# Loading q and k cast, in 14-token pieces, and splitting the score and value PSUM tiles, in an attention kernel with a gated convolution

## The chip, the cores and the metric

The kernel runs on one core of a Trainium2 chip. The metric is the device time of one execution in microseconds (us); lower is better. Times of one kernel vary by about 1% between executions, so kernels that are compared here ran in turn on the same chip, in rounds with the kernel before. Executions at a lower granted TensorE clock or over 1.5% above the fastest of the same kernel count as slow and are left out of the ratios.

Engine names in the profile: PE is TensorE's matmuls and PEld its weight loads, ACT is ScalarE, DVE is VectorE, POOL is GpSimd, SP is SyncE, which issues most transfers. L235 is a line of the kernel's source.

## The reference

Causal attention with 8 batches, 12 heads, 448 tokens and head size 64, then a causal convolution of 5 taps along the tokens as a gate, a value product, and an output product (cut to what matters):

```python
scores = (q @ k.transpose(0, 1, 3, 2)) / sqrt(64)
attn = softmax(where(causal_mask, -1e9, scores))
x = (attn @ v) as [batch, token, head * 64]          # 768 features
gate = sigmoid(sum(conv_w[t] * x shifted by 4 - t for t in range(5)))
out = (gate * (x @ w_val)) @ w_out                    # float32, 8 x 448 x 768
```

## The kernel before

Work goes in 24 groups of four heads (3 groups a batch). Iteration `n` of the main loop computes the scores of group `n`, and the value products, normalisation and convolution of group `n - 1`. From the fourth iteration it also computes a third of the value product of the batch before (`val`), and from the seventh two or three output projections (`next_out`). The engines run their own instruction streams in program order; a semaphore holds an instruction until the tiles that it touches are free or filled.

q and k come in fp32 by whole batches, in 512-byte pieces (two tokens of 64 values), and GpSimd casts them to bf16. A bf16 pair is one 32-bit word, and DVE transposes 32 x 32 blocks of words:

```python
nc.sync.dma_start(out=qk_f[name, b][32 * j:32 * (j + 1), g0:g1].rearrange("p g a c -> p (g a) c"),
                  in_=src[b, h + g0:h + g1].rearrange("h (a p u) d -> p (h a) (u d)", a=7, u=2))
...
nc.gpsimd.tensor_copy(out=t, in_=qk_f[name, n // NG][:, n % NG])                 # cast
...
nc.vector.transpose(out=t.bitcast(U32).rearrange("p (a b u) -> p a u b", u=2, b=32), in_=...)
```

PSUM has one score tile of four banks and one value tile of two:

```python
sc_ps = ps.tile([128, G, 512], FP32, name="sc_ps")     # a bank for each of the four heads
av_ps = ps.tile([128, 2, 512], FP32, name="av_ps")     # a bank for each half of the features
```

The exponential reads the score banks in two instructions of two heads, the convolution of group `n - 1` then reuses the first two banks, and the value product of the batch before reuses `av_ps`:

```python
for hp in range(2):
    nc.scalar.activation(out=pt[:, 2 * hp:2 * hp + 2, ...], in_=sc_ps[:, 2 * hp:2 * hp + 2], func=AF.Exp, scale=D ** -0.5)
...
conv(n - 1, sc_ps[:, 0:2])
...
val(b - 1, g, av_ps)          # 12 matmuls, then one DVE instruction over both halves
```

The main loop, in its order (cut):

```python
for n in range(N + 1):
    load_v(n + 2); ...                       # q and k of the next batches
    # n = 0, 1: 12 loads each of the value weights; n = 2 to 4: 8 each of the output weights (GpSimd)
    # n = 2: DVE reorders all the value weights (order_w)
    scores(n, 0); softmax_numerators(n, 0)   # exponentials, then causal masks on GpSimd
    attend(n - 1)                            # denominators, then value products
    next_out(b - 2, z_ps)
    scores(n, 1); softmax_numerators(n, 1)
    normalize(n - 1)
    next_out(b - 2, den_ps)
    conv(n - 1, sc_ps[:, 0:2])
    ...
    transposes(n + 1); cast_v(n + 1); cast_qk(n + 2)
    val(b - 1, g, av_ps)
```

The softmax here doesn't subtract the row's maximum and nothing guards it: scores larger than these inputs give would overflow.

## Time and profile before

| | before |
|---|---|
| time, median of 2 runs | 291.25 us |
| PE busy | 223.7 us, 77% of the span of 291.6 us |
| start of the convolution of group 1 | 47.88 us |
| groups 5 to 22, a convolution to the next (median) | 9.44 us |
| after the convolution of group 22 | 39.2 us |

The start of each group's convolution is a convenient mark: there is one for each of the 24 groups, and PE executes it in order. Below, "second convolution" is that of group 1. Of the 17 steps from group 5 to 22, two hold one projection more and take 10.4 us, so the 17 take 162.48 us in all. The profiled execution took 293.33 us, 2 us more than the median.

The profile's page, the chain that ended last and the timeline are shown in the prediction. Three rows of its list of waits hold the kernel's three losses. A row has who waited, for whom, the sum in us, how often, and the longest wait:

```profile
PE sc_ps L235 <- ACT pt L184: 25.4, 22, 2.0
PE den_ps L208 <- POOL pt L188: 11.0, 2, 5.8
...
DVE wp L109 <- DMA wv<-in_moe_w_val_dram: 12.0, 3, 6.5
```

The first is the convolution waiting for exponentials: often and short, so it belongs to the steady part. The others are a few long waits, at the start: denominators for masks, and the reordering of the value weights for their transfer.

### The profile page before, as it was taken

Reading aid. Unit: us, or ns where it says so; the run is one execution under the profiler, and the core shown is the slowest. Engines: PE = TensorE matmul, PEld = TensorE weight load, DVE = VectorE, ACT = ScalarE, POOL = GpSimd, SP = SyncE. Lnnn points to the kernel's source line nnn. Section 1 sums busy time; section 2 is a strip of 40 time slices with the busy share of each in tenths; the row PEclk is TensorE's granted clock in tenths of the full one; section 3 lists DMA queues with packets and bytes.
Section 4 is the critical chain, followed back from the end, with each engine's and each line's share of the span. In section 5 each row is a group of like instructions: output and inputs, shape, how many; then the busy total and the mean of one; then the engine's idle time right before and its main releaser. Section 6 shows DMA issues by size and latency. Waiting matters only on the chain.

```text
span 291.6 us, 8183 instructions
## 1 busy us (share of the span) xinstructions
PE 223.7 (77%) x3510; PEld 118.1 (40%) x3510; DVE 121.2 (42%) x184; ACT 141.9 (49%) x177; POOL 146.0 (50%) x240
## 2 busy tenths in 40 slices
PE   0325252797698889888988898889888898899983
PEld 0212121343344445444544454445444454445541
DVE  0404125533643565336534663356335643342100
ACT  1251503533545664556556655575557645712331
POOL 4399399996345436563555355644563463300000
PEclk9999655677989999999999999999999999999999
DMA  7999999999999698979998997967941311111233
GB/s 157 206 214 207 198 202 198 200 197 203 185 175 199 148 204 202 198 162 181 203 213 181 220 179 180 209 141 180 199 104 51 88 56 56 56 45 65 108 148 122
DMA packets 95214, 46.95 MB, mean 161 GB/s; under 512 B 47045, under 2 KB 91589, under 8 KB 95178
## 3 DMA queue, kind: packets, MB, share of 16 engines
q1 hardware_dynamic: 92874, 44.07, 73.0%
q0 software_dynamic: 2304, 2.36, 4.9%
q8 instruction: 27, 0.44, 0.7%
q14 instruction: 9, 0.07, 0.1%
HBM read 37.76 MB, written 11.01 MB: 167 GB/s over the span
## 4 chain that ended last, share of the span: by engine, by line
PE 57%; ACT 11%; DVE 8%; issue 7%; DMA 7%; SPq 6%; POOL 2%; ACTq 0%; DVEq 0%; POOLq 0%
PE av_ps L250 21%; ACT pt L184 10%; PE z_ps L266 9%; PE sc_ps L235 9%; PE av_ps L208 7%; DVE gv L252 7%; PE sc_ps L175 5%; DMA wv<-in_moe_w_val_dram 5%; SPq L61 4%; PE sc_ps L266 3%; PE den_ps L266 2%; DMA vf<-in_v_dram 2%; SPq L82 1%; ACT ob L268 1%; POOL wv L103 0%
## 5 line engine op out<-in xcount | busy, mean ns | idle before, releaser
L184 ACT ACTIVATE pt<-sc_ps 128x1024 bf16<-128x1024 f32 x96 | 93.0, 1021 | 82.8 <-PE sc_ps L175 81.2
L252 DVE SCALAR_TENSOR_TENSOR gv<-gate,av_ps 128x896 bf16<-128x896 f32 x24 | 26.1, 1088 | 110.1 <-PE av_ps L250 110.1
L250 PE MATMUL av_ps<-x,wp 128*128 128x448 bf16 x288 | 63.1, 372 | 0.0
L235 PE MATMUL sc_ps<-x,cwd 32*32 32x448 bf16 x960 | 28.8, 362 | 29.6 <-ACT pt L184 25.4
L194 POOL TENSOR_SCALAR_AFFINE_SELECT pt<-pt 128x512 bf16<-128x512 bf16 x48 | 29.4, 637 | 42.3 <-ACT pt L184 40.0
L250 PEld LDWEIGHTS <-wp 128*128 128x128 bf16 x288 | 27.8, 102 | 33.3 <-issue 12.9
L188 POOL TENSOR_SCALAR_AFFINE_SELECT pt<-pt 128x512 bf16<-128x512 bf16 x24 | 15.4, 640 | 51.0 <-ACT pt L184 51.0
L266 PEld LDWEIGHTS <-gv 128*128 128x128 bf16 x336 | 29.6, 98 | 26.6 <-issue 8.2
L175 PE MATMUL sc_ps<-qt,kt 32*128 32x448 bf16 (+3 forms) x768 | 33.9, 295 | 6.9 <-ACT pt L184 4.9
L239 ACT ACTIVATE gate<-sc_ps 128x896 f32<-128x896 f32 x24 | 22.0, 917 | 26.2 <-PE sc_ps L235 26.2
L235 PEld LDWEIGHTS <-cwd 32*32 32x32 bf16 x960 | 14.5, 91 | 41.3 <-issue 24.5
L266 PE MATMUL z_ps<-wo,gv 128*128 128x384 bf16 x156 | 29.8, 327 | 0.0
L175 PEld LDWEIGHTS <-kt 32*128 32x128 bf16 x768 | 17.7, 98 | 30.0 <-issue 22.1
L208 PE MATMUL av_ps<-pt,vb 128*32 128x448 bf16 (+3 forms) x768 | 28.0, 291 | 2.1 <-DVE gv L252 0.6
L220 DVE TENSOR_TENSOR x<-av_ps,rb 128x896 bf16<-128x896 f32 x24 | 26.2, 1092 | 2.5
L266 PE MATMUL den_ps<-wo,gv 128*128 128x384 bf16 x138 | 26.4, 327 | 0.0
L208 PE MATMUL den_ps<-pt,ones 128*32 128x448 bf16 (+3 forms) x384 | 16.9, 291 | 12.0 <-POOL pt L188 11.0
L268 ACT ACTIVATE ob<-z_ps 128x384 f32<-128x384 f32 x26 | 12.8, 491 | 26.7 <-PE z_ps L266 26.5
L70 POOL CAST qb<-qf 128x896 bf16<-128x896 f32 x24 | 23.0, 958 | 4.9 <-DMA qf<-in_q_dram 4.9
L90 POOL CAST vb<-vf 128x1024 bf16<-128x1024 f32 x24 | 24.9, 1037 | 0.0
L208 PEld LDWEIGHTS <-vb 128*32 128x32 bf16 x768 | 20.3, 102 | 9.8 <-issue 5.6
L70 POOL CAST kb<-kf 128x896 bf16<-128x896 f32 x24 | 22.5, 935 | 3.0 <-DMA kf<-in_k_dram 2.4
(31 smaller groups left out, 143.6 us busy)
## 6 DMA issues: line engine op xcount, KB each, us to landing
out_dram<-ob SPq DMA_DIRECT2D x28, 384.0 KB, 2.8
qf<-in_q_dram SPq DMA_DIRECT2D x28, 336.0 KB, 6.8
kf<-in_k_dram SPq DMA_DIRECT2D x28, 336.0 KB, 6.8
vf<-in_v_dram SPq DMA_DIRECT2D x72, 128.0 KB, 4.1
vf<-in_v_dram SPq DMA_DIRECT2D x24, 64.0 KB, 3.5
qf<-in_q_dram SPq DMA_DIRECT2D x12, 112.0 KB, 2.8
kf<-in_k_dram SPq DMA_DIRECT2D x12, 112.0 KB, 3.2
wv<-in_moe_w_val_dram POOLq DMA_DIRECT2D x24, 48.0 KB, 6.9
```

What stands on the lines that cost most here:

```text
L70: nc.gpsimd.tensor_copy(out=t, in_=qk_f[name, n // NG][:, n % NG])
L90: nc.gpsimd.tensor_copy(out=t, in_=vfs.pop(n))
L175: nc.tensor.matmul(out=sc_ps[:, h, c0:c0 + nq], lhsT=kt[r, e, k0:k0 + 128], rhs=qt[r, e, q0:S], start=e == 0, stop=e == 1, skip_group_chec ...
L184: nc.scalar.activation(out=pt[:, 2 * hp:2 * hp + 2, 512 * stage:512 * (stage + 1)], in_=sc_ps[:, 2 * hp:2 * hp + 2], func=AF.Exp, scale=D ...
L194: nc.gpsimd.affine_select(out=pt[:, :, c:c + 128], in_=pt[:, :, c:c + 128], compare_op=ALU.is_ge, fill=0.0, base=0, pattern=[[0, G], [1, 1 ...
L208: nc.tensor.matmul(out=o, lhsT=w, rhs=pt[:, h, col:col + nq], start=i == 0, stop=i == 3, skip_group_check=True, tile_position=(0, 32 * h))
L220: nc.vector.tensor_tensor(out=x[:, :, 4:S + 4], in0=av_ps[:, :, 0:S], in1=r.unsqueeze(1).to_broadcast([128, 2, S]), op=ALU.mult)
L235: nc.tensor.matmul(out=o[32 * j:32 * (j + 1), dh, 0:S], lhsT=cwd[r, 2 * g + dh, t], rhs=x[r, dh, t:t + S], start=t == 0, stop=t == KW - 1, ...
L239: nc.scalar.activation(out=gate, in_=o[:, :, 0:S], func=AF.Tanh, scale=0.5)
L250: nc.tensor.matmul(out=o[:, dh, 0:S], lhsT=wp_sb[c][:, e:e + 128], rhs=xs[(NG * b + cg) % 8][:, ce, 4:S + 4], start=c == 0, stop=c == NE - ...
L252: nc.vector.scalar_tensor_tensor(out=gv[g][:, :, S * (b % 2):S * (b % 2 + 1)], in0=gates.pop(NG * b + g), scalar=1.0, in1=o[:, :, 0:S], op ...
L266: nc.tensor.matmul(out=o[:, 0:384], lhsT=gvs[p][g][:, dh, 128 * m:128 * (m + 1)], rhs=wo_sb[c][:, f], start=c == 0, stop=c == NE - 1, skip ...
```

## The change

Its intent: take the casts off GpSimd and move fewer and larger pieces, and let PE go on when one half of a PSUM tile is free. In its core (a new head order, four neighbouring heads to a group, the edits that follow from it, and a new order of the first loads are cut):

```diff
-    sc_ps = ps.tile([128, G, 512], FP32, name="sc_ps")
-    av_ps = ps.tile([128, 2, 512], FP32, name="av_ps")
+    sc_ps = [ps.tile([128, 2, 512], FP32, name=f"sc{i}_ps") for i in range(2)]
+    av_ps = [ps.tile([128, 512], FP32, name=f"av{i}_ps") for i in range(2)]
...
+            t = qk_pool.tile([128, T, D], BF16, name=name + "b")          # 4 buffers
+            nc.gpsimd.dma_start(out=t, in_=src[b, G * g:G * (g + 1)].rearrange("h (p s) d -> (h p) s d", s=T))
...
-                out=t.bitcast(U32).rearrange("p (a b u) -> p a u b", u=2, b=32),
+                out=t.bitcast(U32).rearrange("p (b s) -> p s b", s=T),
...
-        nc.vector.tensor_tensor(out=x[:, :, 4:S + 4], in0=av_ps[:, :, 0:S], ...)
+        for dh in range(2):
+            nc.vector.tensor_tensor(out=x[:, dh, 4:S + 4], in0=av_ps[dh][:, 0:S], in1=r, op=ALU.mult)
...
+            nc.vector.scalar_tensor_tensor(                               # inside the loop over dh
+                out=gv[g][:, dh, S * (b % 2):S * (b % 2 + 1)], in0=gates[NG * b + g][:, dh], scalar=1.0,
+                in1=av_ps[dh][:, 0:S], op0=ALU.add, op1=ALU.mult)
...
     for n in range(N + 1):
+        load_qk(n + 3)
...
-            conv(n - 1, sc_ps[:, 0:2])
+            conv(n - 1, sc_ps[0])
```

A partition now holds 14 consecutive tokens of a head (`T = 14`): 3,584 bytes read in one piece and 1,792 written as bf16. Word `b` of block `s` must land at token `14 b + s`, so consecutive words of a transpose are written 14 words, 56 bytes, apart; before they were 8 bytes apart.

More of the change, by code (lines that the diff above doesn't have):

```diff
@@ L19 @@
 N = B * NG
-T = S // 32
+T = 14
 NE = 6
 CHUNKS = ((0, 0, 448, 0), (320, 384, 64, 448), (128, 128, 320, 512), (256, 256, 192, 832))
-V_BUFS = 3
+QK_BUFS, V_BUFS = 4, 3
 @with_exitstack
@@ L31 @@
     sb = ctx.enter_context(tc.tile_pool(name="sb", bufs=1))
-    qk_pool = ctx.enter_context(tc.tile_pool(name="qk", bufs=2))
-    qkb_pool = ctx.enter_context(tc.tile_pool(name="qkb", bufs=2))
+    qk_pool = ctx.enter_context(tc.tile_pool(name="qk", bufs=QK_BUFS))
     tr_pool = ctx.enter_context(tc.tile_pool(name="tr", bufs=2))
@@ L50, with load_qk @@
     qks, vfs, vbs = {}, {}, {}
-    qk_f = {}
-    def load_qk(name, b, j, g0=0, g1=NG):
-        if b >= B:
-            return
-        if (name, b) not in qk_f:
-            qk_f[name, b] = qk_pool.tile([128, NG, 7, 128], FP32, name=name + "f")
-        src = q if name == "q" else k
-        h = NG * j
-        nc.sync.dma_start(
-            out=qk_f[name, b][32 * j:32 * (j + 1), g0:g1].rearrange("p g a c -> p (g a) c"),
-            in_=src[b, h + g0:h + g1].rearrange("h (a p u) d -> p (h a) (u d)", a=7, u=2))
-    def cast_qk(n):
+    def load_qk(n):
         if n >= N:
             return
-        for name in ("q", "k"):
-            t = qkb_pool.tile([128, 7, 128], BF16, name=name + "b")
-            nc.gpsimd.tensor_copy(out=t, in_=qk_f[name, n // NG][:, n % NG])
+        b, g = divmod(n, NG)
+        for name, src in (("q", q), ("k", k)):
+            t = qk_pool.tile([128, T, D], BF16, name=name + "b")
+            nc.gpsimd.dma_start(out=t, in_=src[b, G * g:G * (g + 1)].rearrange("h (p s) d -> (h p) s d", s=T))
             qks[name, n] = t
-    vh = v.rearrange("b (j g) s d -> b g s j d", g=NG)
     v_f = [sb.tile([128, 4, G, D], FP32, name=f"vf{i}") for i in range(V_BUFS)]
@@ L81, in load_v @@
         for c in range(3):
-            nc.sync.dma_start(out=t[:, c], in_=vh[b, g, 128 * c:128 * (c + 1)])
-        nc.sync.dma_start(out=t[64:128, 3], in_=vh[b, g, 384:448])
+            nc.sync.dma_start(out=t[:, c], in_=v[b, G * g:G * (g + 1), 128 * c:128 * (c + 1)].rearrange("h p d -> p h d"))
+        nc.sync.dma_start(out=t[64:128, 3], in_=v[b, G * g:G * (g + 1), 384:448].rearrange("h p d -> p h d"))
         vfs[n] = t
@@ L101, in load_w @@
             h = G - 1 - j if (which and dh) else j
-            r = (NG * h + g) * D + 32 * dh
+            r = (G * g + h) * D + 32 * dh
             nc.gpsimd.dma_start(out=dst[32 * j:32 * (j + 1)], in_=src[r:r + 32])
@@ L106, in order_w @@
         for dh in range(2):
-            w = wv_sb[c].rearrange("p (h g e d) -> p g h e d", h=G, e=2, d=32)[:, :, :, dh]
+            w = wv_sb[c].rearrange("p (g h e d) -> p g h e d", h=G, e=2, d=32)[:, :, :, dh]
             o = wp_sb[c].rearrange("p (g e h d) -> p g e h d", h=G, e=2, d=32)[:, :, dh]
@@ L142, in conv_weights @@
                 out=cwp.rearrange("t (g e) (h d) -> t g e h d", e=2, d=32)[:, :, dh],
-                in_=cwn.rearrange("t (h g e d) -> t g h e d", h=G, e=2, d=32)[:, :, :, dh])
+                in_=cwn.rearrange("t (g h e d) -> t g h e d", h=G, e=2, d=32)[:, :, :, dh])
         for c in range(NE):
@@ L161, in transposes @@
             nc.vector.transpose(
-                out=t.bitcast(U32).rearrange("p (a b u) -> p a u b", u=2, b=32),
-                in_=qks.pop((name, n)).rearrange("p a c -> p (a c)").bitcast(U32).rearrange("p (a u b) -> p a u b", u=2, b=32))
+                out=t.bitcast(U32).rearrange("p (b s) -> p s b", s=T),
+                in_=qks.pop((name, n)).rearrange("p s d -> p (s d)").bitcast(U32).rearrange("p (s d) -> p s d", s=T))
             trs[name, n] = t.rearrange("p (t e) -> p e t", e=2)
@@ L175, in scores @@
                     nc.tensor.matmul(
-                        out=sc_ps[:, h, c0:c0 + nq], lhsT=kt[r, e, k0:k0 + 128], rhs=qt[r, e, q0:S],
+                        out=sc_ps[h // 2][:, h % 2, c0:c0 + nq], lhsT=kt[r, e, k0:k0 + 128], rhs=qt[r, e, q0:S],
                         start=e == 0, stop=e == 1, skip_group_check=True, tile_position=(32 * h, 0))
@@ L185, in softmax_numerators @@
                 out=pt[:, 2 * hp:2 * hp + 2, 512 * stage:512 * (stage + 1)],
-                in_=sc_ps[:, 2 * hp:2 * hp + 2], func=AF.Exp, scale=D ** -0.5)
+                in_=sc_ps[hp], func=AF.Exp, scale=D ** -0.5)
         if stage == 0:
@@ L205, in attend @@
                     r = slice(32 * h, 32 * (h + 1))
-                    o = den_ps[r, q0:S] if dh == 2 else av_ps[r, dh, q0:S]
+                    o = den_ps[r, q0:S] if dh == 2 else av_ps[dh][r, q0:S]
                     w = ones[:, int(ci == 1)] if dh == 2 else vb[:, c, h, 32 * dh:32 * (dh + 1)]
@@ L219, in normalize @@
         nc.vector.transpose(out=r.rearrange("p (a b) -> p a b", b=32), in_=rt.unsqueeze(2).to_broadcast([128, T, 32]))
-        nc.vector.tensor_tensor(out=x[:, :, 4:S + 4], in0=av_ps[:, :, 0:S],
-                                in1=r.unsqueeze(1).to_broadcast([128, 2, S]), op=ALU.mult)
+        for dh in range(2):
+            nc.vector.tensor_tensor(out=x[:, dh, 4:S + 4], in0=av_ps[dh][:, 0:S], in1=r, op=ALU.mult)
     gates = {}
@@ L240, in conv, with val @@
         gates[n] = gate
-    def val(b, g, o):
+    def val(b, g):
         gv = gvs.setdefault(b // 2, [None] * NG)
@@ L249, in val @@
                 e = 128 * (2 * g + dh)
-                nc.tensor.matmul(out=o[:, dh, 0:S], lhsT=wp_sb[c][:, e:e + 128], rhs=xs[(NG * b + cg) % 8][:, ce, 4:S + 4],
+                nc.tensor.matmul(out=av_ps[dh][:, 0:S], lhsT=wp_sb[c][:, e:e + 128], rhs=xs[(NG * b + cg) % 8][:, ce, 4:S + 4],
                                  start=c == 0, stop=c == NE - 1, skip_group_check=True)
-        nc.vector.scalar_tensor_tensor(
-            out=gv[g][:, :, S * (b % 2):S * (b % 2 + 1)], in0=gates.pop(NG * b + g), scalar=1.0,
-            in1=o[:, :, 0:S], op0=ALU.add, op1=ALU.mult)
+            nc.vector.scalar_tensor_tensor(
+                out=gv[g][:, dh, S * (b % 2):S * (b % 2 + 1)], in0=gates[NG * b + g][:, dh], scalar=1.0,
+                in1=av_ps[dh][:, 0:S], op0=ALU.add, op1=ALU.mult)
     obs = {}
@@ L270, in project @@
             nc.sync.dma_start(out=out_rows[2 * S * p + 128 * m:2 * S * p + 128 * (m + 1)], in_=ob)
-    for g in range(NG):
-        for name in ("q", "k"):
-            for j in range(G):
-                load_qk(name, 0, j, g, g + 1)
-        if g == 0:
-            load_v(0)
-            early_consts()
-        if g == 1:
-            load_v(1)
+    load_qk(0)
+    early_consts()
+    load_v(0)
     consts_pool()
-    cast_qk(0)
-    cast_qk(1)
+    load_qk(1)
+    load_v(1)
+    load_qk(2)
     transposes(0)
@@ L304 @@
         b, g = divmod(n, NG)
+        load_qk(n + 3)
         load_v(n + 2)
-        if n == 0:
-            for i in range(8):
-                load_qk("qk"[i % 2], 1, i // 2)
-        else:
-            s = (n - 1) % 3
-            for i in range(8 * s // 3, 8 * (s + 1) // 3):
-                load_qk("qk"[i % 2], (n - 1) // 3 + 2, i // 2)
         if n < 2:
@@ L339 @@
         cast_v(n + 1)
-        cast_qk(n + 2)
         if b > 0:
-            val(b - 1, g, av_ps)
+            val(b - 1, g)
     for g in (1, 2):
@@ L345 @@
         next_out(B - 2, den_ps)
-        val(B - 1, g, av_ps)
-    banks = [z_ps, den_ps, sc_ps[:, 0], sc_ps[:, 1], sc_ps[:, 2], sc_ps[:, 3]]
+        val(B - 1, g)
+    banks = [z_ps, den_ps, sc_ps[0][:, 0], sc_ps[0][:, 1], sc_ps[1][:, 0], sc_ps[1][:, 1]]
     i = 0
```

## The prediction

> **What bounds the kernel now.** I read the engine totals and slices first, then the chain that ended last, then the timeline around one piece of it, then the list of waits, then the start.
>
> ```profile
> PE 223.7 (77%) x3510; PEld 118.1 (40%) x3510; DVE 121.2 (42%) x184; ACT 141.9 (49%) x177; POOL 146.0 (50%) x240
> ...
> PEclk9999655677989999999999999999999999999999
> DMA  7999999999999698979998997967941311111233
> ...
> q1 hardware_dynamic: 92874, 44.07, 73.0%
> q0 software_dynamic: 2304, 2.36, 4.9%
> ```
>
> TensorE (PE) is the busiest engine, at 77%. The 16 DMA engines are full for some 200 us, yet the chain below has no transfer in its steady part: loads run ahead of use. So DMA bounds only the start, where PEclk also drops to 5 tenths.
>
> The chain over one iteration in the steady part (start, length, what):
>
> ```profile
> 113.59 1.06 PE av_ps L208 x32
> 114.65 1.08 PE z_ps L266 x6
> 115.73 0.59 PE sc_ps L175 x16
> 116.33 0.02 issue
> 116.35 0.03 ACT pt L184
> 116.38 0.90 issue
> 117.27 1.03 ACT pt L184
> 118.30 0.04 issue
> 118.34 1.14 PE sc_ps L235 x40
> 119.48 2.39 PE av_ps L250 x12
> 121.87 0.02 issue
> 121.89 1.10 DVE gv L252
> 122.99 0.04 issue
> 123.03 1.06 PE av_ps L208 x32
> ```
>
> The period is 123.03 - 113.59 = 9.44 us. The chain goes twice through another engine. The visit to DVE (gv) is nearly free: scores and denominators run on PE meanwhile. The visit to ScalarE (ACT) is not. The timeline has the two exponentials and the convolution behind them:
>
> ```profile
> 116.35 1.94 ACT L184 ACTIVATE pt<-sc_ps 128x1024 bf16<-128x1024 f32 x2
> ...
> 118.34 1.14 PE L235 MATMUL sc_ps<-x,cwd 32*32 32x448 bf16 x40 [0.96 <-ACT pt L184]
> ```
>
> The convolution writes only heads 0 and 1 of sc_ps, which the first exponential has freed by about 117.3, and still waits for the second, until 118.30: the whole of sc_ps is one tile. The list of waits, limited to 89 to 253 us, has this wait 18 times, 17.3 us in sum.
>
> The start costs more. The timeline there, on POOL (GpSimd), PE and DVE:
>
> ```profile
> 36.43 1.95 POOL L103 DMA_DIRECT2D wv<-in_moe_w_val_dram x4 [4.87 <-DMA wv<-in_moe_w_val_dram]
> ...
> 39.09 0.57 PE L208 MATMUL den_ps<-pt,ones 128*32 128x448 bf16 x4 [5.76 <-POOL pt L188]
> ...
> 44.64 0.48 DVE L109 COPY wp<-wv 128x384 bf16<-128x384 bf16 x2 [4.51 <-DMA wv<-in_moe_w_val_dram]
> ```
>
> POOL issues the weight loads, at most eight in flight, and the causal masks queue behind them. PE waits for the masks; DVE waits for the last weights before it can normalise the second group. PE was busy only 14.3 of the first 47.9 us (busy time by stretch), and the second convolution starts at 47.88.
>
> **What the Trainium skill says.** "DMA: Bandwidth & Descriptors", section "SWDGE vs HWDGE vs iDMA": a cast during a transfer must be issued from GpSimd. So 48 loads move to POOL and into the queue of the weights. Section "Why small descriptors are slow (HBM only)" of that page names a fixed cost per packet. The trace agrees: packet records of queue 1 have 43,008 packets of 512 B at 45.8 ns on average (11.2 B/ns) and 3,072-byte packets at a median of 124 ns (24.8 B/ns). "PSUM — Partial Sum Buffer", section "PSUM bank collisions raise a hardware error", advises to guard by bank and quadrant. This kernel guards four banks as one, and the trace has 0.96 us an iteration for it. "SBUF — State Buffer", section "Door 1: The DMA port swizzle", says that SBUF lines are 16 bytes and want two hits per line. Transposes now write 4-byte words 8 bytes apart, two in a line, and take 636 and 607 ns, no slower than the dense ones (649 and 645 ns). At 56 bytes each word has its own line; no row of this trace shows that cost.
>
> **The change, part by part.**
>
> *Loads.* It removes 80 q and k loads on the SP queue and 48 POOL casts (23.0 + 22.5 = 45.5 us of POOL), and adds 48 POOL loads with one 3,584-byte read per partition. A weight load of 32 rows costs POOL 0.5 us; for 128 rows I estimate 0.5 to 1.2 us, so POOL gains 0 to 20 us. DMA engine time: a cast packet of 1,536 written bytes took 139 ns on average, so one of 1,792 takes about 162 ns (estimate by size). 128 packets over 16 engines make 1.3 us a load, 2.6 us an iteration, against 43,008 x 45.8 ns / 16 / 24 = 5.1 us. With v (43,008 x 20.6 ns, 2.3 us) and the output (3,589 x 144 ns, 1.3 us) the sum falls from 8.7 to 6.2 us an iteration. In the steady part that lies beside other work and is worth nothing by itself, but it lets a shorter period stand.
>
> At the start it counts. q and k of the first group come in two issues rather than eight, and need no cast: first scores at about 7 us, not 10.8. That alone is idle gain, since the masks behind the weight issues come next. The built program shows that eight loads of q and k go into the queue before the first weights, and that the masks of group 0 come after twelve weight issues: the last of these waits for the fourth weight load, itself behind k of group 3. Eight loads at 1.3 us plus the v traffic put that near 19 to 22 us, as before (22.75). After that the weights share the engines only with v, where now they meet a prefetch of whole batches (landings of 6.5 us median). Twelve issues at 0.55 us from 22 put the second masks near 31, not 38.4, and the last weights near 34, not 44.6. I take 10 us off at the second convolution.
>
> *Score tiles.* Two tiles of two banks. The convolution, in the first, waits for one exponential: it can start at 117.41 (end of the first exponential plus 0.04), while PE is free at about 117.35. 0.93 us off each steady iteration. From 89.95 to 252.43 us there are 17.
>
> *Value tiles.* Half the gate product runs beside the second half of its matmuls. Of the DVE visit only about 0.1 us (PE's gap before av_ps) was exposed: 0.1 x 17 more. DVE pays: 896 columns in 1,088 ns and 448 in about 645 make two halves cost 0.2 us more, twice an iteration.
>
> Together 1.03 x 17 = 17.5 us. Period 8.4 us, which is what the PE pieces add up to: 1.07 + 2.38 + 0.56 + 0.62 + 1.0 + 1.08 + 0.56 + 1.08 = 8.35 (start-to-start in the timeline).
>
> *The three iterations from 57.72 to 89.95* last 32.2 us, with both ACT pairs exposed and matmuls at about half clock (val at 3.9 us against 2.39). About 1.2 us less waiting each, and an earlier warm clock worth some 1 us each: 6.5 us.
>
> *The tail.* Seven projections end in score banks and five wait for ACT (3.0 us in the waits). With two tiles, three do: 1.2 us.
>
> *Transposes.* If a line per word doubles the data part, that part grows from about 443 ns (the difference of the 896- and 448-column rows, 1,088 - 645) to 886, so 1.1 us each, an estimate. DVE then has about 5.0 + 0.4 + 1.0 = 6.4 us in 8.4. They come after x and before gv, with some 3 us until the next scores: hidden. At the start 1 us.
>
> Sum: 10 + 17.5 + 6.5 + 1.2 - 1 = 34. From 291.25 that gives 257; I say 258.
>
> **Rivals.** (1) *The strided writes are far worse than double.* Nothing here shows their cost. At 2.5 us each DVE needs 5.4 + 5.0 = 10.4 us an iteration and becomes the bound: 24 x 10.4 plus start and tail, near 300. For it: the diff makes exactly this access worse. Against it: the stream is one word per cycle, and a factor of four is much for a missed line. (2) *POOL, or its queue, becomes the wait.* If each load costs 2 us to issue, POOL has 2.3 (masks) + 1.0 (v cast) + 4 = 7.3 us of 8.4, and masks may come late for the denominators; at the start q and k delay the weights, the gain of 10 goes to zero, and the time is near 268 to 272. Against it: 0.5 us for 32 rows. (3) *ACT takes over the saved wait.* ACT has four exponentials (0.97 pipelined), gate 0.92, two or three copies at 0.5: 5.8 to 6.3 us of 8.4, and the first exponential starts as the scores end, so PE waits at most 0.1: 259 to 260. (4) *The transfers gain nothing since they were hidden.* True in the steady part; with no start gain, 268.
>
> **Range and chances.** The steady gain rests on measured waits (15 to 18 us), the start on my reading of a queue (0 to 15), early iterations 3 to 8. Range 247 to 273. Slower needs rival 1 at its worst.
>
> **What would show it.** Right: no wait of the convolution on ACT beyond 0.1 us, steady period near 8.4, PE over 85% busy, queue 0 with some 11 MB more and near 30% of the engines' span (48 x 128 x 162 ns is 24% of 16 x 258 us), queue 1 near 35%, transposes near 1.1 us, second convolution before 40 us. Wrong: transposes over 2 us with PE waiting for qt, kt or x; POOL loads over 1.5 us with den_ps waiting for masks; the second convolution still near 48 us.

## The result, and the profile after

The kernel after takes 256.97 us (median of 2 runs, 256.54 and 257.39), against 291.25. The ratio is 0.882 (95% interval 0.876 to 0.889). A ratio here is the mean time of one kernel's fast runs over that of the other's of the same rounds, so it is not quite the ratio of the medians quoted.

The page after, in the lines that answer to those of before (the slices are tenths of the span; a queue row has packets, MB and its share of 16 engines' span):

```profile
PE 216.7 (85%) x3510; PEld 114.7 (45%) x3510; DVE 140.5 (55%) x232; ACT 141.2 (55%) x177; POOL 127.9 (50%) x240
...
PEclk9999955899999999999999999999999999999999
DMA  7996949759658678966877786848977211111343
...
q1 hardware_dynamic: 48586, 22.04, 32.6%
q0 software_dynamic: 9216, 13.38, 32.2%
```

PE is up to 85%, and the transfer engines are mostly below nine tenths after the first slices. The chain that ended last, in the steady part:

```profile
104.89 0.87 PE av_ps L194 x32
105.76 1.08 PE z_ps L252 x6
106.84 0.57 PE sc_ps L161 x15
107.41 1.08 PE den_ps L252 x6
108.50 0.03 issue
108.52 1.14 PE sc_ps L221 x39
109.66 2.38 PE av_ps L236 x12
112.04 0.57 PE sc_ps L161 x16
112.61 0.55 PE den_ps L194 x16
113.16 0.87 PE av_ps L194 x32
```

No other engine is left in it. The period is 113.16 - 104.89 = 8.27 us, and PE's own pieces fill it. (The chain counts a piece from the end of the one before, and PE's products overlap; so the value products stand here with 0.87 us and before with 1.06, though the timeline gives 1.05 and 1.06.) The exponentials and the convolution in the timeline:

```profile
115.71 1.94 ACT L170 ACTIVATE pt<-sc_ps 128x1024 bf16<-128x1024 f32 x2
...
116.79 1.14 PE L221 MATMUL sc_ps<-x,cwd 32*32 32x448 bf16 x40
```

The convolution starts 1.08 us after the first of the two exponentials (one takes 1.02), while the second is running; before, it started 1.99 us after. And the waits:

```profile
PE den_ps L194 <- POOL pt L174: 9.0, 4, 3.8
...
DVE wp L95 <- DMA wv<-in_moe_w_val_dram: 4.1, 3, 2.7
...
PE sc_ps L221 <- ACT pt L170: 4.4, 4, 1.1
```

The convolution's 25.4 us of waiting became 4.4, all of it in early iterations that have no projections to fill PE. The wait for masks stayed (11.0 to 9.0 us), that for the value weights fell from 12.0 to 4.1.

By stretches of the two profiled runs (291.6 and 254.8 us), marked by the convolutions (the profiled run of before was 2 us slower than the median, so these gains add up to 36.8 us and not to the 34.3 between the medians):

| stretch | before | after | gain |
|---|---|---|---|
| start to the convolution of group 2 | 57.72 | 48.03 | 9.7 |
| groups 2 to 5 | 32.23 | 27.44 | 4.8 |
| groups 5 to 22 (17 iterations) | 162.48 | 142.41 | 20.1 |
| group 22 to the end | 39.17 | 36.92 | 2.3 |

Four gains of different causes, then. The experiments take them apart.

### The profile page after: what moved, and what is told of

The parts are those of the page before. It is cut to its first block, busy times and chain, and to the rows that moved or that the text cites. A ratio compares the mean times of both kernels' runs of the same rounds, so it can differ in the third digit from the quotient of the medians.

```text
span 254.8 us, 8157 instructions
## 1 busy us (share of the span) xinstructions
PE 216.7 (85%) x3510; PEld 114.7 (45%) x3510; DVE 140.5 (55%) x232; ACT 141.2 (55%) x177; POOL 127.9 (50%) x240
## 3 DMA queue, kind: packets, MB, share of 16 engines
q0 software_dynamic: 9216, 13.38, 32.2%
## 4 chain that ended last, share of the span: by engine, by line
PE 71%; DMA 10%; SPq 8%; POOL 6%; issue 2%; DVE 1%; ACT 1%; POOLq 0%; DVEq 0%
PE av_ps L236 20%; PE z_ps L252 11%; DMA vf<-in_v_dram 10%; PE den_ps L252 10%; PE sc_ps L221 9%; PE sc_ps L161 8%; PE av_ps L194 7%; SPq L68 5%; PE den_ps L194 4%; PE sc_ps L252 3%; SPq L69 3%; POOL pt L180 2%; POOL vb L76 2%; POOL pt L176 1%; POOL pt L174 1%
## 5 line engine op out<-in xcount | busy, mean ns | idle before, releaser
L238 DVE SCALAR_TENSOR_TENSOR gv<-gate,av_ps 128x448 bf16<-128x448 f32 x48 | 29.8, 621 | 52.6 <-PE av_ps L236 52.6
L236 PE MATMUL av_ps<-x,wp 128*128 128x448 bf16 x288 | 58.6, 353 | 0.0
L236 PEld LDWEIGHTS <-wp 128*128 128x128 bf16 x288 | 26.6, 98 | 29.6 <-issue 7.1
L201 DVE STREAM_TRANSPOSE dt<-den_ps 128x448 f32<-128x448 f32 x24 | 15.6, 649 | 29.8 <-PE den_ps L194 29.8
L207 DVE TENSOR_TENSOR x<-av_ps,rb 128x448 bf16<-128x448 f32 x48 | 27.7, 618 | 2.5
L194 PE MATMUL den_ps<-pt,ones 128*32 128x448 bf16 (+3 forms) x384 | 18.1, 291 | 12.2 <-POOL pt L174 9.0
L252 PE MATMUL den_ps<-wo,gv 128*128 128x384 bf16 x138 | 26.4, 327 | 0.0
L147 DVE STREAM_TRANSPOSE qt<-qb 128x448 uint32<-128x448 uint32 x24 | 22.6, 942 | 4.9 <-DMA qb<-in_q_dram 4.9
L147 DVE STREAM_TRANSPOSE kt<-kb 128x448 uint32<-128x448 uint32 x24 | 22.3, 930 | 1.6 <-DMA kb<-in_k_dram 1.6
```

Of the source, the lines that this page charges most:

```text
L147: nc.vector.transpose(out=t.bitcast(U32).rearrange("p (b s) -> p s b", s=T), in_=qks.pop((name, n)).rearrange("p s d -> p (s d)").bitcast( ...
L194: nc.tensor.matmul(out=o, lhsT=w, rhs=pt[:, h, col:col + nq], start=i == 0, stop=i == 3, skip_group_check=True, tile_position=(0, 32 * h))
L207: nc.vector.tensor_tensor(out=x[:, dh, 4:S + 4], in0=av_ps[dh][:, 0:S], in1=r, op=ALU.mult)
L236: nc.tensor.matmul(out=av_ps[dh][:, 0:S], lhsT=wp_sb[c][:, e:e + 128], rhs=xs[(NG * b + cg) % 8][:, ce, 4:S + 4], start=c == 0, stop=c == ...
L238: nc.vector.scalar_tensor_tensor(out=gv[g][:, dh, S * (b % 2):S * (b % 2 + 1)], in0=gates[NG * b + g][:, dh], scalar=1.0, in1=av_ps[dh][:, ...
L252: nc.tensor.matmul(out=o[:, 0:384], lhsT=gvs[p][g][:, dh, 128 * m:128 * (m + 1)], rhs=wo_sb[c][:, f], start=c == 0, stop=c == NE - 1, skip ...
```

## The experiments

The theory when they were planned: the score split gives about 0.93 us a steady iteration, the value split a little, the loads only the start. "Before" in these tables is the kernel before in the same rounds.

### One part at a time

Four kernels: before with only the score tile split; before with only the value tile split; after with both tiles joined again, so only the loads changed; and after with only the score tile joined. Each is a subset of the diff above, for the score tile:

```diff
-    sc_ps = ps.tile([128, G, 512], FP32, name="sc_ps")
+    sc_ps = [ps.tile([128, 2, 512], FP32, name=f"sc{i}_ps") for i in range(2)]
-                in_=sc_ps[:, 2 * hp:2 * hp + 2], func=AF.Exp, scale=D ** -0.5)
+                in_=sc_ps[hp], func=AF.Exp, scale=D ** -0.5)
-            conv(n - 1, sc_ps[:, 0:2])
+            conv(n - 1, sc_ps[0])
```

Only the score tile, expected:

> The kernel before with the score tile split in two, nothing else. My theory (the convolution waits for the second exponential through the shared tile): about 0.95 us off each steady iteration, period 8.5 us, 16 to 17 us in the steady part, some 3 in the early iterations, 1.2 in the tail: 268 to 273 us, with the waits of the convolution on ACT down from 25 us to under 6. Rival (the loads must come down first: q, k, v and output at 8.7 us of DMA time an iteration cannot feed 8.5): period stays over 9 us, 278 us or more, with transposes waiting for casts and casts for loads.

Only the value tile, expected:

> The kernel before with the value tile split by feature half, nothing else. My theory: only PE's gap in front of the value products and the refill of its pipeline after it are exposed, 0.1 to 0.25 us an iteration, 2 to 5 us in all: 286 to 289 us. Rival (the whole DVE visit of 1.10 us counted): 270 us. Other rival (two DVE instructions cost more than the overlap gives): 291 to 294 us.

Only the loads, expected:

> The kernel after with both PSUM tiles joined again, so only the loads, the token order and the transposes change against before. My theory: the start alone gains, second convolution near 39 us instead of 47.9, steady period still 9.4 us: 279 to 283 us. Rival (with fewer packets the steady part runs faster too): under 275 us. Other rival (loads were hidden, gain nothing): 290 us.

The kernel after with the score tile joined, expected:

> The kernel after with the score tile joined again. My theory: the wait of the convolution for the second exponential comes back, 0.9 to 1.0 us an iteration, period 9.2 to 9.3, in all 17 to 22 us: 274 to 279 us. Rival (once the loads are cheap the split matters little): under 265 us.

Measured:

| kernel | median us | ratio to before (95%) | second convolution | groups 2 to 5 | steady period |
|---|---|---|---|---|---|
| before | 292.97 | | 47.9 | 32.2 | 9.44 |
| only scores split | 267.71 | 0.915 (0.911 to 0.920) | 48.3 | 25.7 | 8.51 |
| only values split | 287.73 | 0.984 (0.980 to 0.988) | 48.1 | 31.9 | 9.19 |
| only loads | 283.12 | 0.966 (0.961 to 0.972) | 38.6 | 30.0 | 9.44 |
| after, scores joined | 278.75 | 0.953 (0.949 to 0.958) | 38.5 | 31.9 | 9.19 |
| after | 256.97 (first rounds) | 0.882 (0.876 to 0.889) | 38.7 | 27.4 | 8.26 |

The steady period adds up exactly: the score split takes 9.44 - 8.51 = 0.93 us, the value split 0.25, the loads nothing, and 9.44 - 0.93 - 0.25 = 8.26. The start belongs to the loads alone (9.3 us at the second convolution). The rival that the old loads could not feed a faster period falls: with them and only the score tile split, the period is 8.51, and no wait of PE in the steady part is left in the list of waits. The same row of waits in that run and in the run with only the loads:

```profile
PE sc_ps L235 <- ACT pt L184: 4.3, 4, 1.1
```

```profile
PE sc_ps L221 <- ACT pt L170: 25.4, 22, 2.0
```

The loads alone leave the wait exactly as it was. The run with only scores came 0.3 us below its expected range, since groups 2 to 5 gained 6.5 us rather than 3. The value split gave the upper end of its range, and the run with only loads came 0.1 us above its own. Where its 0.25 us lie, the timelines of the kernels before and after show:

```profile
122.35 0.62 PE L208 MATMUL den_ps<-pt,ones 128*32 128x448 bf16 x16
123.03 1.06 PE L208 MATMUL av_ps<-pt,vb 128*32 128x448 bf16 x32
```

```profile
112.54 0.62 PE L194 MATMUL den_ps<-pt,ones 128*32 128x448 bf16 x16
112.98 1.05 PE L194 MATMUL av_ps<-pt,vb 128*32 128x448 bf16 x32
```

Both groups of products take as long in one kernel as in the other. But the value products begin 0.44 us after the denominators began, not 0.68: that is 0.24 of the 0.25 us. Where PE runs through, the first of them starts 0.02 us after the last denominator product, while that one is still running; where it waits for DVE, it starts 0.26 us after (medians of the steady iterations' start times; they agree within 0.01 us between the runs with the value split, and between those without it). The idle gap before it, 0.06 us, shows only the part of the wait that lies after the end of that product. Besides, the last iteration has no scores to cover the DVE visit: from the convolution of group 22 to the next it went from 8.71 to 7.90 us with the value split, in each kernel that has it.

The three single gains by ratio (8.5 + 1.6 + 3.4 = 13.5%) exceed the 11.8% of the whole. By the table, most of the overlap is in groups 2 to 5, where the score split gained 6.5 us alone and the kernel after only 4.8. There PE waits for masks instead, in the list of waits limited to 38.7 to 75.5 us of the kernel after (3.2 of these 3.5 us lie in groups 2 to 5):

```profile
PE den_ps L194 <- POOL pt L180: 2.0, 5, 0.6
PE den_ps L194 <- POOL pt L174: 1.5, 2, 0.8
```

### Which part of the loads won the start

The loads changed in three ways: larger pieces, a shorter prefetch (three groups ahead instead of whole batches), and the cast on load from the GpSimd queue (with it came the new order of the first loads and of the heads). The first run takes the kernel before with the larger pieces (and so the 56-byte transposes) only:

```diff
-            out=qk_f[name, b][32 * j:32 * (j + 1), g0:g1].rearrange("p g a c -> p (g a) c"),
-            in_=src[b, h + g0:h + g1].rearrange("h (a p u) d -> p (h a) (u d)", a=7, u=2))
+            out=qk_f[name, b][32 * j:32 * (j + 1), g0:g1].rearrange("p g a c -> p g (a c)"),
+            in_=src[b, h + g0:h + g1].rearrange("h (p s) d -> p h (s d)", s=14))
```

> The kernel before with the 14-token pieces and the 56-byte transposes, but loaded as before: on the SP queue, whole batches ahead, fp32, cast on GpSimd. It parts the size of the pieces from the cast on load and the depth of prefetch. Theory A (the engines were slow with 512-byte packets and the weights queued behind them): second convolution at 40 to 43 us, not 47.9, and 283 to 287 us; steady period still 9.44. Theory B (what the change wins at the start is the shorter prefetch, three groups instead of two batches): second convolution after 46 us, 289 us or more.

The next two take the shorter prefetch, with 512-byte pieces and then with the larger ones:

```diff
-        if n == 0:
-            for i in range(8):
-                load_qk("qk"[i % 2], 1, i // 2)
-        else: ...
+        for i in range(8):
+            load_qk("qk"[i % 2], (n + 3) // 3, i // 2, (n + 3) % 3, (n + 3) % 3 + 1)
```

> The kernel before, with q and k still in fp32, 512-byte pieces, on the SP queue and cast on GpSimd, but loaded group by group three groups ahead, as the kernel after does, instead of by whole batches. It parts the depth of prefetch from the cast on load. Theory depth (the weights queued behind a whole batch): second convolution at 41 us or earlier, 281 to 285 us. Theory cast (the engines are full at some 205 to 215 GB/s of written bytes whatever the pieces, and the cast halves what q and k write): second convolution at 44 to 48 us, 287 to 292 us.

> As the run before with 14-token pieces and 56-byte transposes as well; against the run with the loads alone only the cast on load and the queue differ. Theory cast: second convolution still at 44 us or later, 287 to 293 us, and 195 to 220 GB/s while the engines are full. Theory pieces and depth together: second convolution near 39 us, 280 to 284 us.

| kernel | median us | ratio to before (95%) | second convolution | landing of a value weight load, median us |
|---|---|---|---|---|
| before | 292.7 to 293.3 | | 47.9 | 6.9 |
| large pieces | 294.22 | 1.006 (0.999 to 1.013) | 48.7 | 7.7 |
| short prefetch | 289.96 | 0.988 (0.982 to 0.993) | 44.5 | 5.7 |
| short prefetch, large pieces | 288.77 | 0.981 (0.972 to 0.989) | 43.7 | 5.4 |
| only loads (with the cast on load) | 283.12 | 0.966 (0.961 to 0.972) | 38.6 | 5.1 |

(The profile of the run with both fell in a slow run; its second convolution is from that one. Its clock was 0.99, and the neighbouring run agrees within 0.8 us.)

Larger pieces alone win nothing. From 5 to 45 us, with the engines full, the kernel before moves 205 GB/s in 19,017 packets and the one with large pieces 215 GB/s in 11,108:

```profile
DMA packets 19017, 8.19 MB, mean 205 GB/s; under 512 B 8245, under 2 KB 19009, under 8 KB 19014
```

```profile
DMA packets 11108, 8.61 MB, mean 215 GB/s; under 512 B 8825, under 2 KB 9593, under 8 KB 11106
```

So the packet count is not what filled the engines: 42% fewer packets moved 5% more. By the packet records of these 40 us, the q and k packets did move faster (14.6 bytes per ns at 3,584 bytes, 11.3 at 512), but of the packets that are left 7,726 are those of v, of 256 bytes, which no run changed. The weights even land later, 7.7 us against 6.9. The Trainium skill, "DMA: Bandwidth & Descriptors", section "Queues, rings and completion order", says that an engine takes turns between its queues packet by packet, so larger packets of one queue could delay the other; but with the short prefetch the larger pieces land the weights earlier (5.4 against 5.7), so these runs don't show it.

The shorter prefetch brings the second convolution 3.4 us forward, and the cast on load from GpSimd's queue 5.1, of 9.3 in all. The 0.8 of the pieces on top is no more than kernels with the same loads differ by (37.8 to 38.7 in five profiles), and the intervals of those two ratios overlap. The run with large pieces fell in the range of theory B, and the one with the short prefetch in that of the cast: each cause is part of it, the cast step the larger. The GB/s above count written bytes, and the cast halves what q and k write (22.0 MB to 11.0): from 20 to 40 us the transfer engines' share (packets that overlap count twice, so it can pass 1) is 1.15 with short prefetch and large pieces, 0.79 with the cast on load. But that step also removes GpSimd's 45.5 us of casts and most issues on the SP queue and changes the order of the first loads, so that the halved bytes are the cause is likely and not shown.

### Do the 56-byte writes matter?

The kernel after with dense transposes, `"p (s b) -> p s b"`: the tokens of q and k come out in the wrong order.

> The kernel after with the transposes of q and k written densely; tokens come out in the wrong order, so the result is wrong on purpose, with the same instructions otherwise. My theory (the 56-byte writes cost 0.3 us each but lie beside other work): transposes at about 640 ns instead of 936, time 255.5 to 257.5 us, steady period still 8.26. Rival (they delay the scores): 250 us or less.

Measured: 257.62 us median, ratio 0.879 (0.872 to 0.885), against 0.882 (0.876 to 0.889) with the strided writes; steady period 8.26. The rows of the transposes (out, in, count, busy us, mean ns, idle before), of the kernel after and of this run:

```profile
L147 DVE STREAM_TRANSPOSE qt<-qb 128x448 uint32<-128x448 uint32 x24 | 22.6, 942 | 4.9 <-DMA qb<-in_q_dram 4.9
L147 DVE STREAM_TRANSPOSE kt<-kb 128x448 uint32<-128x448 uint32 x24 | 22.3, 930 | 1.6 <-DMA kb<-in_k_dram 1.6
```

```profile
L147 DVE STREAM_TRANSPOSE qt<-qb 128x448 uint32<-128x448 uint32 x24 | 15.2, 635 | 5.7 <-DMA qb<-in_q_dram 5.7
L147 DVE STREAM_TRANSPOSE kt<-kb 128x448 uint32<-128x448 uint32 x24 | 14.5, 606 | 1.1 <-DMA kb<-in_k_dram 1.1
```

The stride costs 0.31 us an instruction, 15 us of DVE in all, and none of it is on the path of the steady part (the period is the same); the times differ by less than their intervals. One caution: the comparison with the reference passed although q and k were scrambled. Products of 64 numbers near 0.1, over 8, are near 0.01, so all exponentials are near 1 and the order of q and k hardly shows. That check can't vouch for the new token order; the derivation (token `14 b + s`) has to.

What the stride costs by itself, in 26 more transposes of the same 448 words at the end of the kernel after, to scratch, two for each distance:

```diff
+    [nc.vector.transpose(out=scatter(4), in_=swi) for _ in range(2)]        # words 16 bytes apart; likewise 1, 2, 3, ...
+    [nc.vector.transpose(out=weave(14), in_=swi[:, 0:14]) for _ in range(2)] # 56 bytes, blocks interleaved
```

> The kernel after with 26 more transposes of the same 128x448 words at its end, to scratch, two for each distance between written words: 4, 8, 12, 16, 20, 32, 56, 64 and 80 bytes with each block in its own region, and 28, 56, 64 and 112 bytes with the blocks interleaved as q and k are (at 28 bytes only 7 blocks). If two words in a 16-byte line are what counts: 4, 8 at about 640 ns and every distance from 16 bytes on at about 936, with 12 between. Rival (the cost grows with distance): 80 and 112 bytes clearly above 936. Rival (interleaving collides, not distance): blocks apart at 56 bytes near 640 ns. The total time says nothing here.

The run was correct (one execution, state unknown; 263.75 us, the time says nothing). The rows for 4, 8, 12, 16, 56 and 80 bytes, blocks apart, and for 56 bytes interleaved; a row has minimum, median and maximum in ns:

```profile
L331 DVE STREAM_TRANSPOSE sw<-swi x2: 637/641/645, 237.3 to 238.0; 128x448 uint32<-128x448 uint32 x2
L332 DVE STREAM_TRANSPOSE sw<-swi x2: 646/652/657, 238.6 to 239.3; 128x448 uint32<-128x448 uint32 x2
L333 DVE STREAM_TRANSPOSE sw<-swi x2: 781/784/787, 240.0 to 240.8; 128x448 uint32<-128x448 uint32 x2
L334 DVE STREAM_TRANSPOSE sw<-swi x2: 974/976/979, 241.6 to 242.7; 128x448 uint32<-128x448 uint32 x2
...
L337 DVE STREAM_TRANSPOSE sw<-swi x2: 947/948/948, 247.8 to 248.8; 128x448 uint32<-128x448 uint32 x2
...
L339 DVE STREAM_TRANSPOSE sw<-swi x2: 1110/1111/1112, 251.7 to 252.8; 128x448 uint32<-128x448 uint32 x2
...
L341 DVE STREAM_TRANSPOSE sw<-swi x2: 939/940/941, 255.2 to 256.2; 128x448 uint32<-128x448 uint32 x2
```

At 4 and 8 bytes, with two words or more in 16, the time is the same to 0.01 us; 12 bytes lies between, and from 16 bytes the cost is a step of about 0.3 us: 976 at 16, 996 at 20 and at 32, 948 at 56, 930 at 64. Interleaving changes nothing (940 against 948). It isn't quite flat: 80 bytes took 1,111, as the rival of distance had it, and 112 bytes interleaved 986, which neither theory explains.

### The wait that is left at the start

In the kernel after, the weight loads of an iteration still stand before its masks in GpSimd's stream. First, move them behind the masks and the v cast; second, move DVE's reordering of the value weights (`order_w`, at n = 2) behind the second normalisation as well:

```diff
-        if n < 2: ... load_w(0, c)                 # at the head of the iteration
-        if n == 2: ... order_w(c)                  # stays in the first of the two runs
...
         transposes(n + 1)
         cast_v(n + 1)
+        if n == 2: ... order_w(c)                  # second run only
+        if n < 2: ... load_w(0, c)                 # and the output weights likewise
```

> The kernel after with the weight loads of an iteration issued after its masks and the v cast instead of before them. My theory (the masks of the first groups wait behind the weight issues on GpSimd): first convolution near 19 us instead of 26.4, no waits of den_ps on masks over 1 us, 248 to 254 us. Rival (DVE's ordering of the weights, which the second normalisation waits for, is the true bound and the weights now come later): second convolution still at 38 us or later, 256 us or more.

> As the run before, and the ordering of the value weights on DVE moved behind the second normalisation and the transposes of the fourth group. My theory: neither masks nor DVE hold the second convolution: it starts before 32 us, and 240 to 249 us. Rival (the first value products then wait for the weights and give it back): as the run before within 2 us.

| kernel | median us | ratio to before (95%) | first, second convolution |
|---|---|---|---|
| after | 256.97 | 0.882 (0.876 to 0.889) | 26.4, 38.7 |
| masks first | 254.96 | 0.870 (0.863 to 0.877) | 21.0, 41.9 |
| masks first, reordering late | 248.46 | 0.850 (0.844 to 0.856) | 20.8, 31.5 |

(The profile of the run with masks first fell in a slow run; its convolutions are from that one. The median lies between the range of the theory, 248 to 254 us, and that of the rival, 256 or more; one wait for masks of 2.4 us was left.) Masks first alone mends most of the first convolution (21.0, not the 19 expected) and not the second, for which PE waits 11.1 us on DVE. There the reordering waits 8.8 us in all for weights that come later: the rival was right about that step. Two of its copies also took 3.3 us instead of 0.27, see the last section. With both moved, the second convolution starts at 31.5 us, and time and start are in the expected ranges. In the kernel after, the issues aren't all that holds the masks: before its weight issues GpSimd waited 10.7 us in all, 13 times, for q and k to land, now that these share its queue.

The last run adds two things: the value weights and half the output weights in one load of 128 rows instead of four of 32, and the last projections in turn from the two score tiles:

```diff
+        if not (which and dh):
+            nc.gpsimd.dma_start(out=dst, in_=src.rearrange("(g h e r) f -> g e h r f", h=G, e=2, r=32)[g, dh])
+            return
...
-    banks = [z_ps, den_ps, sc_ps[0][:, 0], sc_ps[0][:, 1], sc_ps[1][:, 0], sc_ps[1][:, 1]]
+    banks = [z_ps, den_ps, sc_ps[0][:, 0], sc_ps[1][:, 0], sc_ps[0][:, 1], sc_ps[1][:, 1]]
```

> The kernel after with the weights issued after the masks, the ordering of the weights late (as in the run with both, 248.5 us), the 36 weight loads that can be so issued merged into 9 of 128 rows, and the last projections alternating between the two score tiles. My theory: GpSimd's 0.5 us an issue held the masks of the first groups, so early iterations shrink from about 10.4 to about 8 us, and the last waits on ACT (1.7 us) go: 239 to 245 us. Rival (the engines' bytes hold the early iterations, not the issues): 246 to 248 us.

Measured: 243.94 us, ratio 0.832 (0.827 to 0.837), correct; 5% below the kernel after, and in the theory's range. Only part of the theory held. The second convolution came at 26.9 us, since GpSimd's weight issues of an iteration took 2.1 us instead of 5.8; so the issues had bound it. But the third came 12.1 us later: merged weight loads took 9.5 us to land (median, four times the bytes), and the reordering and so the third normalisation waited for them, so their landing bound that iteration (the rival put it down to the bytes, which no run separates). The last waits on ACT (1.7 us in the kernel after) are gone from the list, and group 22 to the end took 34.7 us instead of 36.9: half of the 4.5 us against the run before.

## Why the prediction was right

The time was 258 us predicted, 256.97 measured. Its steps:

- **Score tiles.** Predicted 0.93 us a steady iteration from the wait in the timeline; measured 0.93 with that part alone. Right, and by the mechanism named.
- **Value tiles.** The mechanism is right, the size off: "only about 0.1 us" was taken from the idle gap in front of the value products. The term was 0.25, since the wait also cost PE the overlap of those products with the one before (they start 0.26 us after its start, not 0.02), and the last iteration gave 0.8 us that was not counted, because no scores cover the visit there. So the steady part gave 20.1 us, not 17.5, and the period is 8.26, not 8.4.
- **Loads at the start.** Predicted 10 us at the second convolution, measured 9.2 (47.88 to 38.66). The queue was read rightly: masks of group 0 at 19.96 us ("19 to 22"), of group 1 at 32.24 ("near 31"), last weights reordered from 33.9 ("near 34"). The prefetch of whole batches, which it named, is a third of it (3.4 us); 5.1 came with the cast on load, whose parts no run separates. One step failed: "The trace agrees" on a cost per packet. It set a mean in SBUF loads (45.8 ns, 11.2 B/ns) beside a median in output stores (124 ns; their mean is 143.5, 21.4 B/ns), and its own 256-byte packets of v, at 20.6 ns, moved 12.4 B/ns, faster than those of 512. The section that it cites holds putting descriptors together to be worth it only at 256 bytes or less; and 3,584-byte packets alone saved no time (ratio 1.006). So the term for the start came out nearly right in part by luck. First scores came at 9.5 us, not 7: k landed late, its transpose ended at 8.4, and the convolution weights went before the scores on DVE and PE. That costs nothing, as the prediction said.
- **Groups 2 to 5.** Predicted 6.5 us, measured 4.8. The clock gave more than the 3 us assumed: PE's busy time there fell by 4.1 us (26.0 to 22.0; `val` took 2.44 us instead of 3.7 to 4.1), with a granted clock of 1.00 instead of 0.84. The waits gave less: PE's idle time fell by 0.7 us (6.2 to 5.5), not by three times 1.2, as the denominators now waited 3.2 us for masks behind the weight issues. That is the term that was mis-sized. How early PE runs at full speed differed from kernel to kernel, and no run set it: with the short prefetch PE was busy 27.2 us there, at a recorded clock of 0.90.
- **Tail.** 2.3 us against 1.2: the waits that it counted fell from five and 3.0 us to three and 1.7, as predicted, and the last iteration's 0.8 came on top.
- **Transposes.** 0.94 us against 1.1, and hidden, as predicted.
- **GpSimd.** A load of q or k costs 0.55 us to issue, inside 0.5 to 1.2. Queue 0 took 32% of the engines' span ("near 30%"), queue 1 33% ("near 35%").
- **Rivals.** None took over: DVE at 55%, no wait of PE in the list of waits of the steady part, for masks or for ACT. Rival 4 stands for the steady part, as the prediction had it: the loads alone leave the period at 9.44. The old loads, 8.7 us of packet time an iteration by the prediction's sum, still fed a period of 8.51, running ahead; nothing shorter was tried with them.

Over-estimates (start, early groups) and under-estimates (steady part, tail) nearly cancelled, so the total is closer than its terms.

## What to carry to other kernels

Where one engine releases a tile in pieces and another waits for a piece, make the tile as small as the piece: the gain here was the length of the wait (0.93 of 0.96 us) in every iteration in which that wait closes the loop, and the timeline shows it before anything is built. Where engines overlap consecutive instructions, as PE does here, measure a wait from the start of the instruction before it and not from its end. A read of the engines' rate while they are full says nothing about the cost of a packet; change the packets and nothing else before it is named as the cause. When the steady part is full, look in the start for long instruction streams (weight issues, reorderings) in front of a small one that others wait for.

## What the Trainium skill lacked or had wrong

- "DMA: Bandwidth & Descriptors", section "Why small descriptors are slow (HBM only)": not wrong, but read too widely in the prediction. It says that putting descriptors together is only worth it at 256 bytes or less, and here 3,584 instead of 512 bytes for q and k moved 215 instead of 205 GB/s and saved no time (ratio 1.006). The same page has no rate for a load that casts: 3,584 bytes read and 1,792 written took a median of 154 ns a packet, against 124 ns for 3,072 plain bytes stored.
- The same page, section "Anatomy of one DMA — SWDGE (gpsimd) path", calls the time to generate descriptors on GpSimd "small, variable" and gives no figure. Here an issue took 0.50 us for 32 rows, 0.55 us for 128 rows of q or k and 0.69 us for 128 rows of the value weights, so one load of 128 weight rows held GpSimd for a third of what four of 32 did.
- "SBUF — State Buffer", section "Door 1: The DMA port swizzle": two hits per 16-byte line agrees with DVE's 32-bit writes here up to 64 bytes, but no size is given: 0.64 us dense, 0.65 at 8 bytes, 0.78 at 12, 0.98 at 16, 0.93 to 1.00 from 20 to 64, 1.11 at 80.
- The same page, section "Who interferes with whom": a DVE copy in a two-port mode and GpSimd block each other for the whole instruction. It doesn't say for how long a run of instructions can hold it: in the run with the reordering late, one copy of a kind that takes 0.27 us took 3.27 us (35.64 to 38.91 us) while GpSimd ran four masks and a cast back to back (35.59 to 38.75). Five more copies in four other runs took 3.1 to 3.4 us and also ended 0.15 us after such a run of GpSimd. Cause inferred from the overlap, not tested; that these copies use a two-port mode is assumed:

```profile
L95 DVE COPY wp<-wv x12: 270/330/3272, 32.1 to 39.1; 128x384 bf16<-128x384 bf16 x12
```
